# A network in six visits: half of the hidden width for one block of tokens at a time

## The chip, the cores and the metric

One core of a Trainium2 chip runs the kernel. Its engines are TensorE (PE; its weight loads are listed as PEld), VectorE (DVE), ScalarE (ACT), GpSimd (POOL) and SyncE (SP, which here issues nearly all transfers). The metric is the device time of one execution in microseconds (us), lower is better. Times of parts come from one profiled execution, counted from the start of its span.

## What is computed

Attention with a threshold, then eight experts of which each token takes one, then one network shared by all tokens:

```python
def _moe_ref(x, expert_emb, tau, w1, w2):            # N, D, E, F = (2304, 512, 8, 1024)
    ...
    for e in range(E):
        mask = expert_idx == e
        h = np.maximum(x[mask] @ w1[e], 0.0)
        out[mask] = gate_w[mask, None] * (h @ w2[e])
    return out.astype(np.float32)

def _moe2_ref(x, w_in, w_out, alpha):                # d_model, d_ff = 512, 2048
    h = x @ w_in
    g = np.maximum(h, 0.0) + alpha * np.minimum(h, 0.0)
    return (g @ w_out).astype(np.float32)
```

The weights of the experts and of the network arrive as 64-bit floats. Every matrix product is made of three with halves of lower precision (high x high, high x low, low x high), so most operands are split into a high and a low half.

## The kernel before

**Stages.** Attention runs to 349 us, the experts to about 625, the network to the end. The experts go step by step (`g` from 0 to 64, eight steps to an expert): a step loads staged weights `stg`, splits them (`wsplit`, L1118 to L1133), and multiplies (`l`, activation `h`, output `y`). An expert's result leaves as `yT` to `yt_d` in DRAM.

**The network's data.** Its hidden width of 2048 is 16 chunks of 128, `f`, in 8 pairs, `i`. A pair isn't multiplied directly: seven products, `PROD` = 1, 2, 6, 7, 5, 3, 4, of combined weights with combined tokens take the place of eight. The combined weights ("factors") of all 8 pairs are made in the experts, which leave DVE and POOL some room: `conv` converts half a pair of `w_in` (ScalarE L1594, DVE L1596 to L1605, POOL L1611), `sums` makes four sums on POOL (L1646 to L1649), and `factor` splits each of the seven (ScalarE L1661, POOL L1662) and stores it to `ws` in DRAM, 56 stores of 256 KB. `y2["early"]` gives the step `g` at which each is written out. The tokens' combinations come from `diff` (L1692 to L1698) and `split` (ScalarE L1683 high, DVE or POOL L1684 low) out of `raw`, read back by `fetch` from `yt_d`.

**The network's order.** Three blocks of 768 tokens (`q`), each in two halves (`hf`), go through all 8 pairs: 24 iterations. An iteration makes the seven products in two banks, `ha` and `hb` (L1759), each from weights `wr` loaded from `ws` one iteration ahead. `held` copies `ha` on ScalarE (L1764: v, w, d) since the bank goes on to be added to; `act` adds it to `hb` on DVE (`c`, L1773) and applies the activation, in block 0 by two ScalarE operations (L1777, L1778) and a join on DVE (L1785), later by two on DVE (L1782, L1783); then ScalarE makes the high half `gh` (L1789) and POOL the low half `gl` (L1790). `f2mm` multiplies the chunk's `gh` and `gl` with `w_out` (L1817 to L1819) into six banks `o`, between the products of the next iteration. After a block's last pair, `evac` scales the six banks by the gate into `os` (four buffers, ScalarE L1829 and DVE L1827), and `put` stores them to the tokens' rows (POOL, L1833).

**Conversions in the network.** `w_out` has 16 chunks; one is converted in the experts, 15 in block 0, one each four `cstep` calls, on the same engines with POOL L1616 and L1617 at the end.

**Order.** Each engine runs its instructions as written; `after`, `tick` and `cstep` in the text place the secondary work between products.

## Time and profile before

| | us |
|---|---|
| Median of three runs (1050.13 to 1053.92) | 1052.05 |
| The profiled execution | 1048.41 |
| Its span | 1046.5 |
| Attention, from the span's start | 349 |
| Experts, about | 276 |
| Network and end, about | 421 |

The profiled execution's time holds 1.9 us around its span. In rows of a timeline the columns are start, duration, engine, line, operation, output and inputs, and in brackets the engine's idle time ahead of it with what ended that; the duration of merged rows holds all of them. Matmuls overlap, so their starts tell more than their durations. In groups by line, "xN" is the count, then the busy time and the mean of one in ns.

### The profile page before, as it was taken

How to read it: one execution, taken by the hardware profiler on the slowest of the kernel's cores; microseconds unless marked ns; L12 is line 12 of the kernel's file. 1: busy time of each engine (PE TensorE's matmuls, PEld its weight loads, DVE VectorE, ACT ScalarE, POOL GpSimd, SP SyncE). 2: the span in 40 equal slices, each digit the busy share in tenths (PEclk: the TensorE clock that was granted, in tenths of full speed). 3: DMA queues.
4: the chain of work that ended last, by engine and by line, in shares of the span. 5: the costliest groups of instructions: out<-in, count | busy, mean ns of one | idle time of the engine just before them, and what ended most of it. 6: DMA issues, size and time to landing. Idle time of an engine off the chain costs nothing.

```text
span 1046.5 us, 18304 instructions
## 1 busy us (share of the span) xinstructions
PE 972.2 (93%) x6099; PEld 900.1 (86%) x6099; DVE 765.9 (73%) x1426; ACT 590.6 (56%) x1373; POOL 642.4 (61%) x640
## 2 busy tenths in 40 slices
PE   7999999899998699998998978998889999999995
PEld 6999999899997699998988966887778899889984
DVE  7999999999999588888886737866766434754342
ACT  6899999799996446665555535554452221422121
POOL 6988898899997226667875645654564222532223
PEclk9999999999999799999989989998989999999998
DMA  3333547533541766999999577554445334453331
GB/s 80 103 88 85 158 128 211 153 100 107 152 143 41 284 233 236 299 321 257 263 253 266 161 229 190 205 171 151 134 139 171 113 118 157 155 158 111 115 82 64
DMA packets 117049, 172.29 MB, mean 165 GB/s; under 512 B 23737, under 2 KB 57529, under 8 KB 116945
## 3 DMA queue, kind: packets, MB, share of 16 engines
q1 hardware_dynamic: 113344, 161.43, 52.4%
q0 software_dynamic: 3456, 9.46, 2.4%
q8 instruction: 51, 0.84, 0.3%
q14 instruction: 54, 0.43, 0.1%
q10 hardware_dynamic: 144, 0.13, 0.0%
HBM read 119.09 MB, written 43.04 MB: 155 GB/s over the span
## 4 chain that ended last, share of the span: by engine, by line
PE 53%; DVE 16%; issue 8%; DMA 8%; ACT 7%; POOL 7%; SPq 0%; POOLq 0%; ACTq 0%; DVEq 0%
PE ha L1759 7%; PE hb L1759 6%; PE s L622 5%; PE o L1819 5%; PE o L1818 5%; PE o L1817 5%; PE t L658 4%; DMA stg<-in_moe_w_dram 4%; PE l L1220 4%; DVE p L645 2%; DVE mx L629 2%; PE v L702 2%; PE m L721 2%; PE v L703 2%; PE y L1252 2%
## 5 line engine op out<-in xcount | busy, mean ns | idle before, releaser
L1790 POOL TENSOR_TENSOR gl<-c,gh 128x384 fp32r<-128x384 f32 x96 | 106.7, 1114 | 221.6 <-ACT gh L1789 134.2
L441 POOL TENSOR_TENSOR ptl<-x,pth 128x512 fp32r<-128x512 f32 x97 | 124.8, 1287 | 6.8
L1759 PE MATMUL ha<-x,wr 128*128 128x384 f32 x576 | 118.4, 341 | 4.4 <-ACT c L1778 2.8
L645 DVE SCALAR_TENSOR_TENSOR p<-s,mx,e 128x576 f32<-128x576 f32 x144 | 116.6, 812 | 7.2 <-ACT e L638 3.2
L1220 PE MATMUL l<-x,w 128*128 128x256 f32 (+6 forms) x744 | 121.4, 313 | 0.0
L1759 PEld LDWEIGHTS ha<-x,wr 128*128 128x128 f32 x576 | 104.1, 189 | 13.6 <-ACT c L1778 3.3
L1819 PE MATMUL o<-wo,gl 128*128 128x512 f32 x288 | 115.3, 400 | 0.4 <-POOL gl L1790 0.4
L1818 PE MATMUL o<-wo,gh 128*128 128x512 f32 x288 | 115.2, 400 | 0.0
L629 DVE TENSOR_REDUCE mx<-s 128x1 f32<-128x576 f32 x144 | 108.5, 754 | 8.1 <-PE s L622 5.1
L1220 PEld LDWEIGHTS l<-x,w 128*128 128x128 f32 x744 | 113.7, 193 | 0.6
L1817 PE MATMUL o<-wo,gh 128*128 128x512 f32 x288 | 114.1, 396 | 0.0
L658 PE MATMUL t<-ident,p 128*128 128x128 f32 (+1 forms) x720 | 111.8, 276 | 2.2 <-ACT x L684 0.9
L638 ACT ACTIVATE e<-s,mx 128x576 f32<-128x576 f32 x144 | 106.3, 739 | 6.6 <-DVE mx L629 6.0
L1759 PE MATMUL hb<-x,wr 128*128 128x384 f32 x432 | 91.1, 347 | 15.3 <-DVE c L1773 15.3
L1251 PE MATMUL y<-h,w 128*128 128x256 f32 (+6 forms) x256 | 84.9, 332 | 11.2 <-ACT h L1203 7.3
L1759 PEld LDWEIGHTS hb<-x,wr 128*128 128x128 f32 x432 | 78.3, 194 | 18.7 <-DVE c L1773 18.1
L1252 PE MATMUL y<-h,w 128*128 128x256 f32 (+6 forms) x256 | 82.7, 323 | 6.4 <-DVE h L1204 6.2
L658 PEld LDWEIGHTS t<-ident,p 128*128 128x128 f32 (+1 forms) x720 | 80.8, 137 | 8.3 <-ACT x L684 2.2
L622 PE MATMUL s<-ks,qs 128*128 128x288 f32 x256 | 82.7, 338 | 2.9 <-ACT qs L529 1.4
L1789 ACT CAST gh<-c 128x384 fp32r<-128x384 f32 x96 | 49.1, 511 | 62.3 <-DVE c L1783 55.7
L1253 PE MATMUL y<-h,w 128*128 128x256 f32 (+6 forms) x256 | 81.5, 318 | 0.0
L1773 DVE TENSOR_TENSOR c<-hb,d 128x384 f32<-128x384 f32 x24 | 13.4, 557 | 91.4 <-ACT d L1764 91.4
(252 smaller groups left out, 2568.1 us busy)
## 6 DMA issues: line engine op xcount, KB each, us to landing
wr<-ws SPq DMA_DIRECT2D x168, 256.0 KB
stg<-in_moe_w_dram SPq DMA_DIRECT2D x34, 512.0 KB
stg<-in_moe_w_dram SPq DMA_DIRECT2D x15, 1024.0 KB
ws<-wr SPq DMA_DIRECT2D x56, 256.0 KB
kx<-ks SPq DMA_DIRECT2D x60, 144.0 KB
xd<-zt SPq DMA_DIRECT2D x33, 256.0 KB
raw<-in_moe_w_in_dram SPq DMA_DIRECT2D x16, 512.0 KB
raw<-in_moe_w_out_dram SPq DMA_DIRECT2D x16, 512.0 KB
```

The costliest lines, as they stand in the source:

```text
L441: lambda: nc.gpsimd.tensor_tensor(lo, raw, hi.bitcast(F32), op=ALU.subtract))
L622: nc.tensor.matmul(s[:, hf, 0:288], lt, st[nm, a][:, hf * 288:(hf + 1) * 288], start=(j == 0 and x == 0), stop=(j == n - 1 and x == 1))
L629: nc.vector.tensor_reduce(out=mx[:, 0:1], in_=st["s", t][:, :, 0:288], op=ALU.min, axis=AX.XY)
L638: nc.scalar.activation(e, st["s", t][:, :, 0:288], AF.Exp, bias=st["mx", t][:, 0:1], scale=-1.0)
L645: nc.vector.scalar_tensor_tensor(out=p.rearrange("q (a b) -> q a b", a=2), in0=st["s", t][:, :, 0:288], scalar=st["mx", t][:, 2:3], in1=st ...
L658: nc.tensor.transpose(m[0:w, j * n + i * 128:j * n + (i + 1) * 128], st["p", t][:, c * 128:c * 128 + w], ident)
L1220: nc.tensor.matmul(m[:, 0:n], w[:, a, c], st["x"][:, b, c, 0:n], start=(i == 0), stop=(i + 1 == len(terms)))
L1759: nc.tensor.matmul(m, w[:, a, k], x[:, b, k], start=start and n == 0, stop=n + 1 == len(terms), skip_group_check=not start)
L1790: nc.gpsimd.tensor_tensor(gl, c, gh.bitcast(F32), op=ALU.subtract)
L1817: nc.tensor.matmul(m, gh[:, ts], WO[f][:, 0, :], start=(n[0] == 1), stop=False)
L1818: nc.tensor.matmul(m, gh[:, ts], WO[f][:, 1, :], start=False, stop=False)
L1819: nc.tensor.matmul(m, gl[:, ts], WO[f][:, 0, :], start=False, stop=(n[0] == KF2))
```

## The change

**Visits.** The network runs in six visits: block 0, 1, 2 with pairs 0 to 3, then block 2, 1, 0 with pairs 4 to 7, again 24 iterations with the same products. Between the two visits of block 2 the tokens stay; for blocks 0 and 1 the first visit's banks are scaled and stored in DRAM as `part` (12 stores of 256 KB), and read back and added in the second. The token block moves four times in place of two.

**Weights.** In the experts only pairs 0 to 3 get their factors; for 4 to 7 the converted `w_in` is stored as `wa_d` (four stores of 512 KB), and visits 1 to 3 load it and make the factors (`factors`: four sums on DVE, seven high halves on ScalarE, seven low ones on POOL, seven stores, with a ring `wf` of three tiles). Of `w_out`, four chunks are converted in the experts, four in visit 0 and eight in visits 1 to 3 (`wout`). `wr` has six buffers in place of eight, loaded five products ahead.

**Experts.** Conversions come every 2.6 steps in place of 3.4, with scratch tiles of the token pool; low halves of `w2` go to POOL every second step in place of every fourth; the fetch of block 0 stands ahead of step 54, its splits spread from step 56 on. `yt_d` holds two d-chunks of a token side by side, so a token's run is longer, and `split` reads every second word.

**A scheduler in the source.** Secondary steps are chains: a list of steps, each with an engine and a rough cost. After each product and each `f2mm`, `tick` gives every engine room and writes out what fits, at most one engine's steps of a chain at a time; "N" is an empty step, "W" a condition, "S" a transfer. `finish` writes out the rest of a chain where its result is due.

```diff
-CVG = {False: [17 * i // 5 for i in range(KF2 + 1)], True: [4 * i for i in range(15)] + [59, 61]}
+CVG = {False: [21 * i // 8 for i in range(KF2 + 4)], True: [4 * i for i in range(15)] + [59, 61]}
...
-NR = 8
-AHEAD = {0: 0, 4: 1, 5: 2, 6: 3, 7: 4}
+NR = 6
+VISITS = ((0, 0), (1, 0), (2, 0), (2, 1), (1, 1), (0, 1))
+NV = 4
+NQH = NP // 2
+NWO = 12
...
-    yt_d = dram.tile([128, KD, NT + CAPS_NEAR[0]], F32, name="yt_d")
+    yt_d = dram.tile([128, 2, NT + CAPS_NEAR[0], KD // 2], F32, name="yt_d")
+    wa_d = dram.tile([NQH, 128, 2 * DM], F32, name="wa_d")
+    part = dram.tile([4 * HT, 128, DM], F32, name="part")
...
-            eng = nc.gpsimd if not general and which == 2 and g % 4 == 1 and g > 8 else nc.vector
+            eng = nc.gpsimd if not general and which == 2 and g % 2 == 1 and g > 8 else nc.vector
...
-        def factor(i, p, eng):
-
-            t, flat, home = wtile(i, p)
+        def factor(i, p):
+
+            t, flat, home = wtile(y2["wf"], "wf", i, p)
             src = SUM[i][p]
             hi, lo = (t[:, x].rearrange("p (k j) -> p k j", k=2) for x in range(2))
             nc.scalar.copy(hi, src)
-            eng.tensor_tensor(lo, src, hi.bitcast(F32), op=ALU.subtract)
+            yield
+            nc.gpsimd.tensor_tensor(lo, src, hi.bitcast(F32), op=ALU.subtract)
+            yield
             nc.sync.dma_start(home, flat)
 
...
-            nc.sync.dma_start(t.rearrange("p (k n) -> p k n", k=KD), yt_d[:, :, n0:n0 + HB])
+            nc.sync.dma_start(t.rearrange("p (a n) -> p a n", a=2), yt_d[:, :, n0:n0 + HB, :].rearrange("p a n b -> p a (n b)"))
...
+            src = src.rearrange("p (n k) -> p k n", k=KD // 2)
+            XS[p] = t = pools[p].tile([128, 2, KD // 2, HB], F32R, tag=f"x{p}", name=f"x{p}")
...
+        for i in range(NQH):
+            g0 = 10.5 * i + 4.0
+            at(g0, lambda i=i: y2.update(sm=sums(i, WA[i])))
+            for x in range(4):
+                at(g0 + 0.5 * x, lambda x=x: y2["sm"][x](G))
+            for x, p in enumerate((1, 2, 4, 6, 7, 5, 3)):
+                f = run(lambda i=i, p=p: factor(i, p))
+                for y in range(3):
+                    at(g0 + 2.2 + 1.1 * x + 0.5 * y, f)
...
+        at(53.1, lambda: fetch(0, 0))
+        at(53.2, lambda: fetch(0, 1))
+        g0 = 56.0
+        for x, (kind, p, e) in enumerate((("s", 1, V), ("d", 1, G), ("s", 2, G), ("d", 3, V), ("d", 2, G), ("s", 7, V),
+                                          ("s", 6, V), ("s", 5, G), ("d", 4, G))):
...
+        for x in range(NR - 1):
+            at(59.0 + 0.7 * x, weights)
...
-        os_p = npool("os", bufs=4)
+        os_p = npool("os", bufs=2 * HT)
...
+        y2["wf"] = npool("wf", bufs=3)
...
+        def chain(order, steps, name=None, later=0):
+            chains.append({"order": (order, now[0]), "steps": list(steps), "at": now[0] + later, "name": name})
+            chains.sort(key=lambda c: c["order"])
+
+        def finish(name):
+            for x in [c for c in chains if c["name"] == name]:
+                while x["steps"]:
+                    x["steps"].pop(0)[2]()
+                if x in chains:
+                    chains.remove(x)
...
+        def tick(us):
+
+            now[0] += 1
+            for e in room:
+                room[e] = min(room[e] + us, 1.2)
+            for x in list(chains):
+                last = None
+                while x["steps"] and x["at"] < now[0]:
+                    e, cost, fn = x["steps"][0]
+                    if last not in (None, e) or room.get(e, 1) <= 0 or e == "W" and not fn():
+                        break
+                    x["steps"].pop(0)
+                    if e == "W":
+                        continue
+                    fn()
+                    if e in room:
+                        room[e] -= cost
+                    last = e
+                    if e == "N":
+                        break
+                if last is not None:
+                    x["at"] = now[0]
+                if not x["steps"] and x in chains:
+                    chains.remove(x)
+
...
+        def prod(v, i, p, m, start):
+            finish(("x", p))
...
                                  skip_group_check=not start)
+            if y2["wnext"][0] < len(y2["wseq"]):
+                vv, ii, _ = y2["wseq"][y2["wnext"][0]]
+                finish(("f", VISITS[vv][1] * NQH + ii))
+            y2["weights"]()
...
+            if v < 3:
+                first = [("A", 0.5, lambda: A.activation(u, m, AF.Relu, scale=-1.0)),
+                         ("A", 0.5, lambda: A.activation(c, m, AF.Relu))]
+                join = [("V", 0.87, lambda: V.scalar_tensor_tensor(
+                    out=c, in0=u, scalar=y2["na"][:, f:f + 1], in1=c, op0=ALU.mult, op1=ALU.add))]
...
+            chain(0, first + join + [("A", 0.52, halves), ("P", 1.12, low)], ("g", v, f, hf), 1)
...
+        def evac(v, hf, j, m):
+            q, h = VISITS[v]
+            tt = (2 * q + hf) * HT + j
+            g = y2["gs"][:, tt, 1:2].bitcast(F32)
+            last = v == NVIS - 1
+            loaded = h and q != VISITS[2][0]
+            if loaded:
+                o = O.pop(("part", tt))
+                V.scalar_tensor_tensor(out=o, in0=m, scalar=g, in1=o, op0=ALU.mult, op1=ALU.add)
...
+            if h:
+                if last:
+                    put(tt, o)
+                else:
+                    chain(1, [("P", 1.28, lambda: put(tt, o))])
...
+                chain(1, [("S", 0, lambda: nc.sync.dma_start(part[tt], o))], ("part", tt))
...
+        def partial(v, hf):
+            q, h = VISITS[v]
+            for j in range(HT):
+                tt = (2 * q + hf) * HT + j
+                finish(("part", tt))
+                O["part", tt] = o = os_p.tile([128, DM], F32, tag="os", name="os")
+                nc.sync.dma_start(o, part[tt])
...
+                finish(("g", v, f, hf))
+                finish(("wo", f))
...
+            kinds = [("V", 0.75), ("V", 0.75), ("V", 1.2), ("A", 0.65), ("V", 0.5), ("V", 0.75), ("P", 1.55), ("P", 1.4)]
+            chain(3, [("W", 0, lambda: len(open_) < 2), ("S", 0, load)] + [("N", 0, nothing)] * 3 + [("A", 0.67, begin)]
+                  + [(e, t, lambda k=k: nth(k + 1)) for k, (e, t) in enumerate(kinds)], ("wo", c))
...
+        def factors(i):
+
+            x = {}
+
+            def load():
+                made.append(i)
+                x["wa"] = wa = y2["wa"].tile([128, 2, DM], F32, tag="wa", name="wa")
+                nc.sync.dma_start(wa.rearrange("p x n -> p (x n)"), wa_d[i - NQH])
+
+            def nth(k):
+                if k == 0:
+                    x["sums"] = y2["sums"](i, x["wa"])
+                x["sums"][k](V)
+
+            def next_(k):
+
+                if k < 7:
+                    x[k] = t, _, _ = y2["wtile"](y2["wf"], "wf", i, PROD[k])
+                    A.copy(t[:, 0].rearrange("p (k j) -> p k j", k=2), SUM[i][PROD[k]])
+                    did("A", 0.42)
+                if 1 <= k < 8:
+                    h, l = (x[k - 1][0][:, y].rearrange("p (k j) -> p k j", k=2) for y in range(2))
+                    P.tensor_tensor(l, SUM[i][PROD[k - 1]], h.bitcast(F32), op=ALU.subtract)
+                if k >= 2:
+                    nc.sync.dma_start(x[k - 2][2], x[k - 2][1])
+                if k == 8:
+                    made.remove(i)
+
+            steps = [("W", 0, lambda: not made), ("S", 0, load)] + [("N", 0, nothing)] * 3
+            steps += [("V", 0.8, lambda k=k: nth(k)) for k in range(4)] + [("N", 0, nothing)]
+            for k in range(9):
+                steps += [("P", 0.95, lambda k=k: next_(k)), ("N", 0, nothing)]
+            chain(4, steps, ("f", i))
...
+                    chain(2, [("S", 0, lambda: fetch(VISITS[v + 1][0], 0)), ("S", 0, lambda: fetch(VISITS[v + 1][0], 1))]
+                          + [("N", 0, nothing)] * 5 + [("P", 2.15, lambda: diff(1, P)), ("V", 1.0, lambda: diff(3, V)),
+                                                       ("P", 2.15, lambda: diff(2, P))], "fetch")
...
+        work = {0: [("o", NV + x, x) for x in range(NQH)], 1: [("f", NQH, 0), ("f", NQH + 1, 2)] + [("o", 8 + x, x) for x in range(3)],
+                2: [("f", NQH + 2, 0), ("f", NQH + 3, 2), ("o", 11, 0), ("o", 12, 3)], 3: [("o", 13, 0), ("o", 14, 1), ("o", 15, 2)]}
...
+                if (v, i) != (NVIS - 1, NQH - 1):
+                    f2mm(v, (f0,), 0)
+        f2mm(v, (f0,), 1)
+        f2mm(v, (f1,), 1)
+        f2mm(v, (f0, f1), 0)
```

**DVE in the network's first iterations.** In before (`f<-f`, `f<-raw,f`, `r` are the five operations of a conversion; `c<-hb` is the addition, `c<-u,na,c` the join):

```order
L1773 TENSOR_TENSOR c<-hb,v 128x384
L1596 TENSOR_SCALAR f<-f 128x512
L1598 TENSOR_SCALAR f<-f 128x512
L1600 SCALAR_TENSOR_TENSOR f<-raw,f 128x512
L1785 SCALAR_TENSOR_TENSOR c<-u,na,c 128x384
L1604 TENSOR_SCALAR r<-f 128x512
L1605 SCALAR_TENSOR_TENSOR r<-raw,r 128x512
L1773 TENSOR_TENSOR c<-hb,d 128x384
L1785 SCALAR_TENSOR_TENSOR c<-u,na,c 128x384
```

and after, in the first visit, where `cr` is the raw `w_out`:

```order
L1891 TENSOR_TENSOR c<-hb,v 128x384
L1613 TENSOR_SCALAR r<-f 128x512
L1614 SCALAR_TENSOR_TENSOR r<-cr,r 128x512
L1897 SCALAR_TENSOR_TENSOR c<-u,na,c 128x384
L1606 TENSOR_SCALAR f<-f 128x512
L1607 TENSOR_SCALAR f<-f 128x512
L1891 TENSOR_TENSOR c<-hb,d 128x384
L1609 SCALAR_TENSOR_TENSOR f<-cr,f 128x512
L1897 SCALAR_TENSOR_TENSOR c<-u,na,c 128x384
L1613 TENSOR_SCALAR r<-f 128x512
L1891 TENSOR_TENSOR c<-hb,w 128x384
L1897 SCALAR_TENSOR_TENSOR c<-u,na,c 128x384
```

The three long operations of a conversion, which stood in a row, stand in two pieces with an addition or a join between.

**ScalarE where the last factors are due,** before in an iteration of block 1:

```order
L1764 COPY v<-ha 128x384
L1789 CAST gh<-c 128x384
L1764 COPY w<-ha 128x384
L1789 CAST gh<-c 128x384
L1764 COPY d<-ha 128x384
L1789 CAST gh<-c 128x384 x2
```

and after, in the third iteration of visit 3 (`wf` are the high halves of pair 7's factors):

```order
L1878 COPY v<-ha 128x384
L1913 CAST gh<-c 128x384
L2041 CAST wf<-wa 128x256 x2
L2041 CAST wf<-sum 128x256 x4
L2041 CAST wf<-wa 128x256
L1878 COPY w<-ha 128x384
L1913 CAST gh<-c 128x384
```

Seven copies have come in between the copies "v" and "w" of one iteration, in one piece.

**POOL at the end,** before:

```order
L1790 TENSOR_TENSOR gl<-c,gh 128x384 x3
L1833 DMA out_dram<-os,gs 2304x512 x6
L1790 TENSOR_TENSOR gl<-c,gh 128x384 x31
L1833 DMA out_dram<-os,gs 2304x512 x6
```

and after:

```order
L1950 DMA out_dram<-os,gs 2304x512
L1918 TENSOR_TENSOR gl<-c,gh 128x384 x11
L1950 DMA out_dram<-os,gs 2304x512 x3
L1918 TENSOR_TENSOR gl<-c,gh 128x384
L1950 DMA out_dram<-os,gs 2304x512 x3
```

One low half, which stood ahead of all six indirect stores, now stands behind three of them.

## Rows read from the trace of the kernel before

**Rows 1.** Busy time by stretch: start, end, length, each engine's busy us, granted clock, DMA.
```profile
460.00:600.00 140.00, 130.06 (x870) 125.88 (x869) 112.86 (x170) 76.70 (x181) 98.65 (x94) 0.95 0.92 248
...
608.00:615.00 7.00, 0.41 (x4) 0.17 (x2) 1.82 (x3) 2.90 (x6) 0.88 (x2) 0.71 1.03 307
...
640.00:776.00 136.00, 123.72 (x573) 108.01 (x573) 100.81 (x127) 69.99 (x145) 77.59 (x60) 0.95 0.50 168
776.00:905.00 129.00, 126.94 (x621) 113.89 (x622) 65.49 (x101) 34.62 (x68) 45.45 (x41) 0.99 0.45 139
```

**Rows 2.** Waits of TensorE, 349 to 640 us: total us, times, longest.
```profile
PE y L1251 <- ACT h L1203: 7.3, 2, 6.6
...
PE y L1251 <- ACT yT L1259: 3.9, 1, 3.9
```

**Rows 3.** Waits of TensorE, 640 us to the end.
```profile
PE hb L1759 <- DVE c L1773: 14.6, 7, 3.2
```

**Rows 4.** Timeline of TensorE in the network.
```profile
625.52 1.22 PE L1759 MATMUL ha<-x,wr 128*128 128x384 f32 x6
...
640.99 1.72 PE L1759 MATMUL ha<-x,wr 128*128 128x384 f32 x6 [2.85 <-ACT c L1778]
...
708.78 1.23 PE L1759 MATMUL ha<-x,wr 128*128 128x384 f32 x6
...
717.40 2.29 PE L1759 MATMUL hb<-x,wr 128*128 128x384 f32 x6 [3.22 <-DVE c L1773]
...
730.80 1.23 PE L1759 MATMUL ha<-x,wr 128*128 128x384 f32 x6
...
790.32 1.20 PE L1759 MATMUL ha<-x,wr 128*128 128x384 f32 x6
...
996.48 1.23 PE L1759 MATMUL ha<-x,wr 128*128 128x384 f32 x6
...
1012.19 1.23 PE L1759 MATMUL ha<-x,wr 128*128 128x384 f32 x6
...
1025.82 0.39 PE L1817 MATMUL o<-wo,gh 128*128 128x512 f32 x1
...
1033.79 0.39 PE L1819 MATMUL o<-wo,gl 128*128 128x512 f32 x1
```

**Rows 5.** Groups by line and shape, 640 us to the end.
```profile
L1785 DVE SCALAR_TENSOR_TENSOR c<-u,na,c 128x384 f32<-128x384 f32 x30 | 23.1, 771 | 8.1 <-ACT c L1778 7.9
...
L1773 DVE TENSOR_TENSOR c<-hb,v 128x384 f32<-128x384 f32 x23 | 12.7, 553 | 23.4 <-PE hb L1759 22.1 <-POOL gl L1790 0.9 <-ACT v L1764 0.4
...
L1605 DVE SCALAR_TENSOR_TENSOR r<-raw,r 128x512 f32<-128x512 uint32 x14 | 9.7, 692 | 0.5
...
L1616 POOL TENSOR_TENSOR f<-f,wo 128x512 f32<-128x512 f32 x14 | 19.0, 1357 | 0.0
```

**Rows 6.** Groups by line and shape, 363 to 626 us.
```profile
L1662 POOL TENSOR_TENSOR wr<-sum,wr 128x256 fp32r<-128x256 f32 x32 | 32.5, 1030 | 4.8 <-ACT wr L1661 4.5 <-issue 0.3
...
L1661 ACT CAST wr<-sum 128x256 fp32r<-128x256 f32 x32 | 12.7, 414 | 5.5 <-POOL sum L1647 5.5
```

**Rows 7.** The chain that ended last, 600 to 760 us: start, us, what.
```profile
598.00 8.17 DMA raw<-yt_d
...
629.34 10.16 DMA raw<-in_moe_w_out_dram
...
702.70 2.77 DMA wr<-ws
...
747.85 4.83 DMA wr<-ws
```

**Rows 8.** One of the splits, by line and shape, 640 us to the end.
```profile
L1684 DVE TENSOR_TENSOR x<-raw,x 128x768 fp32r<-128x768 f32 x8 | 10.5, 1332 | 7.1 <-ACT x L1683 7.1
```

**Rows 9.** Timelines of POOL and DVE at the end.
```profile
1038.47 0.97 POOL L1833 DMA_INDIRECT out_dram<-os,gs  x1 [0.57 <-ACT os L1829]
...
1034.72 0.75 DVE L1827 TENSOR_SCALAR os<-o,gs 128x512 f32<-128x512 f32 x1 [2.47 <-DMA out_dram<-os,gs]
```

More of the change, by code (lines that the diff above doesn't have):

```diff
@@ L1509, in experts @@
         ba = iter(()) if general else bases()
-        ahead, early = y2["ahead"], y2["early"]
+        early = y2["early"]
         todo = []
@@ new lines, in conv @@
+            steps = [x[2] for x in cvsteps(CV.pop((which, c)), f, r, hl)]
+            for group in ((0,), (1, 2, 3), (4,) if hl is not None else ()):
+                for x in group:
+                    steps[x]()
+                if group:
+                    yield
+            for x in steps[5 if hl is not None else 4:]:
+                x()
+            cvload()
+            if hl is None:
+                i, half = divmod(c, 2)
+                yield
+                if half == 0:
+                    WA[i] = y2["wa"].tile([128, 2, DM], F32, tag="wa", name="wa", bufs=2)
+                nc.gpsimd.tensor_tensor(WA[i][:, half], f.bitcast(F32), r.bitcast(F32), op=ALU.add)
+                if half and i >= NQH:
+                    yield
+                    nc.sync.dma_start(wa_d[i - NQH], WA.pop(i).rearrange("p x n -> p (x n)"))
@@ L1823, in evac, with low @@
-        def evac(tt, m, odd):
-            o = os_p.tile([128, DM], F32, tag="os", name="os")
-            g = y2["gs"][:, tt, 1:2].bitcast(F32)
-            if odd:
-                nc.vector.tensor_scalar(out=o, in0=m, scalar1=g, scalar2=None, op0=ALU.mult)
-            else:
-                nc.scalar.activation(o, m, AF.Copy, scale=g)
-            late.append(lambda: put(tt, o))
+                A.copy(gh, c)
+                G[v, f, hf] = gh, gl
+            def low():
+                gh, gl = G[v, f, hf]
+                P.tensor_tensor(gl, c, gh.bitcast(F32), op=ALU.subtract)
@@ new lines, in f2mm @@
+        def f2mm(v, fs, hf):
+            if v < 0:
+                return
+            q, h = VISITS[v]
+            joined = q == VISITS[2][0]
+            n = O.setdefault((q, hf), [0])
+            full = KF2 if joined else KF2 // 2
+            gs = []
+            for f in fs:
+                finish(("g", v, f, hf))
+                finish(("wo", f))
+                gs.append((f, *G.pop((v, f, hf))))
+            first, n[0] = n[0] == 0, n[0] + len(fs)
+            for j in range(HT):
+                if first:
+                    n.append(ps_o.tile([128, 512], F32, tag="o", name="o"))
+                m = n[1 + j]
+                ts = slice(j * 128, (j + 1) * 128)
+                for x, (f, gh, gl) in enumerate(gs):
+                    nc.tensor.matmul(m, gh[:, ts], WO[f][:, 0, :], start=first and x == 0, stop=False)
+                    nc.tensor.matmul(m, gh[:, ts], WO[f][:, 1, :], start=False, stop=False)
+                    nc.tensor.matmul(m, gl[:, ts], WO[f][:, 0, :], start=False, stop=n[0] == full and x + 1 == len(gs))
+                if n[0] == full:
+                    evac(v, hf, j, m)
+            if n[0] == full:
+                O.pop((q, hf))
+            tick(2.08 * len(fs))
@@ new lines, in xdiff_after_six @@
+        def xdiff_after_six():
+            chain(2, [("N", 0, nothing)] * 2 + [("P", 2.15, lambda: (finish(("x", 6)), diff(4, P)))], ("d", 4))
+        work = {0: [("o", NV + x, x) for x in range(NQH)], 1: [("f", NQH, 0), ("f", NQH + 1, 2)] + [("o", 8 + x, x) for x in range(3)],
+                2: [("f", NQH + 2, 0), ("f", NQH + 3, 2), ("o", 11, 0), ("o", 12, 3)], 3: [("o", 13, 0), ("o", 14, 1), ("o", 15, 2)]}
+        xsplit(3, "V")
+        xsplit(4, "V")
+        for v, (q, h) in enumerate(VISITS):
+            for i in range(NQH):
+                pair = h * NQH + i
+                f0, f1 = 2 * pair, 2 * pair + 1
+                if i:
+                    pv, g0, g1 = v, f0 - 2, f1 - 2
+                else:
+                    pv = v - 1
+                    pp = VISITS[pv][1] * NQH + NQH - 1
+                    g0, g1 = 2 * pp, 2 * pp + 1
+                for kind, x, when in work.get(v, ()):
+                    if when == i:
+                        (wout if kind == "o" else factors)(x)
+                if h and q != VISITS[2][0] and i == NQH - 2:
+                    partial(v, 1)
+                if h and q != VISITS[2][0] and i == NQH - 1:
+                    partial(v, 0)
```

428 lines of the change are left out of this document (216 added, 212 removed).

## The prediction

> **What bounds the kernel now.** I read four views, in this order. The table of busy time by stretch comes first, to see which part has room. Up to 349 us (attention) the change touches nothing. Of the rest, the experts (349 to 625) run with the DMA engines nearly full (0.92 from 460 to 600) and TensorE idle for 10 us there; one 7 us stretch, from 608 to 615, has TensorE busy for 0.41 us only [rows 1]. In the network the DMA engines are half used (0.50, 0.45), and TensorE is idle mostly in its first third: 12.3 us of 136, then 2.1 of 129 [rows 1]. So the experts are bound by what they load, with a hole at the hand-over, and the network by TensorE with waits early.
>
> Second, the waits of TensorE say who is late. In the experts it is the activation (7.3 us in two, one of them the hole) and the copies that empty the output banks (3.9) [rows 2]; in the network DVE's first addition of an iteration, `c`, 14.6 us in seven waits [rows 3].
>
> Third, the timeline of TensorE gives the network's loss, by the starts of its iterations. A quiet one takes 1012.19 - 996.48 = 15.71 us. The network starts at 625.52 and its last matmul at 1033.79, so it ends near 1034.1: 408.6 us against 24 x 15.71 = 377.0, a loss of 31.6 us [rows 4]. The last 36 matmuls (512 wide) start 0.228 apart, 35 spacings in 1033.79 - 1025.82 = 7.97 us; so the 36 of an iteration take 8.2 and its 42 narrow ones the other 7.5, six of them 1.07. The first nine iterations carry the loss: 790.32 - 625.52 = 164.8 against 9 x 15.71 = 141.4, less 27 x 0.228 = 6.2 (the first has no work of a predecessor), so 29.6 [rows 4]. A wait costs more than itself: the iteration from 708.78 to 730.80 lost 6.3 us, while TensorE stood 3.22; right after, six matmuls take 2.29 instead of 1.23 [rows 4]. I count 1.5 to 2 times each wait for that reason.
>
> Fourth, the operations: the conversions of `w_out` are what fills DVE and POOL there. an activation's addition takes 0.55 us and its join 0.77 on DVE; of a conversion's five operations there the last takes 0.69, and POOL's first 1.36 [rows 5]. Before puts three of the five back to back, and the other two right ahead of a `c` for which TensorE waits.
>
> **The change part by part.** The time is worked out against the profiled run, 1048.41 us; the median of the runs is 3.6 above it.
>
> *Network, iterations without special events.* Matmuls are the same in number and shape. `w_out` conversions come one or two DVE operations at a time between the `c` additions, as the order of DVE shows. DVE's sum for an iteration in the first two visits comes to 10 to 12 us (three additions and four joins at 0.55 and 0.77 [rows 5], conversions, splits), below 15.71, so a clump no longer sets the pace. I give each of the 19 iterations without an event 0.3 us: 6 us.
>
> *First iteration.* Before it took 640.99 - 625.52 = 15.47 us, where 15.71 - 6.2 = 9.5 would do: 6.0 lost [rows 4]. The chain shows why: a `raw` of `w_out` that landed after 10.16 us [rows 7], and its conversion on ScalarE ahead of an activation. After puts three empty steps between load and conversion, so ScalarE isn't held; 2 us (0.6 if all is hidden, 6 if not).
>
> *Moves of the token block.* Four instead of two. The second move of before cost at most the 2.1 us that TensorE was idle from 776 to 905 [rows 1]; after starts both loads ahead of the last iteration: 1.5 each, 6 us (0 to 12).
>
> *`w_out` chunk 7 (visit 1, first iteration).* It is four operations short when its product comes, and `finish` writes them out there. Behind p2 DVE must do `c` 0.55, a join 0.77, then two more at up to 0.69, then POOL one of 1.36 [rows 5]: some 4 us during which TensorE stands; with the slower matmuls 6 (2 to 7).
>
> *Factors of pair 7 (visit 3, third iteration).* `finish` writes seven ScalarE copies in one piece, ahead of `held` "w", through a ring of three tiles. Copy 3 waits for copy 0 (0.41), its low half (1.03) [rows 6] and its store; copy 6 for the same again. No row shows a store of 256 KB in the network; the nearest are loads of 256 KB there, 2.77 and 4.83 us [rows 7]. With 2.77, twice (0.41 + 1.03 + 2.77) = 8.4 us of ScalarE, plus "w" itself and two operations before; TensorE reaches the product that needs "w" 7.3 us after it has done p1 (three products of 1.07 and eighteen wide matmuls): a wait of 2.3, with 4.83 of 6.4. I take 4 with the slow matmuls (2 to 9). Stores stand on SP ahead of 26 loads of `wr`, but those are five products early.
>
> *The rest of the factors and the partial sums.* 28 stores of 256 KB leave the experts; what SP issues in the network grows from 52.7 to 71.0 MB, counted in its order. With half of the DMA time free there [rows 1], I take the 18.3 MB at nothing; what hides them is the five products by which `wr` is loaded ahead. Without that cover they would be 18.3 MB at the 168 GB/s of 640 to 776 [rows 1], 109 us, all on the path; the nearest row, TensorE idle for 2.1 of 129 us with 0.45 of the DMA time used [rows 1], is far nearer to nothing. The last conversion, just before visit 4: 0.5.
>
> So the network loses 6 + 2 + 6 + 6 + 4 + 0.5 = 24.5 against 31.6: 7 us won (bounds: 12 to 36 lost).
>
> *Experts.* DVE gets three conversions more and 14 low halves fewer, POOL 28 factor lows (1.03 [rows 6]) and 16 sums fewer and 14 low halves more: both no longer. SP's order shows equal bytes between the `yt_d` stores up to about step 45, so 460 to 540 stays as it is; after that there are fewer. The hole at 608 to 615 comes out of the fetch of the first block (8.17 us in the chain [rows 7]), then the splits, ahead of the last activations on ScalarE. After fetches two to three steps earlier and spreads the splits over seven. The hole is 6.6 us [rows 2], some 10 with the slow matmuls behind it; I count 7 of these as won, and 2 of a 3.9 us wait for the copies that empty the banks [rows 2]: 9 us (3 to 17).
>
> *End of the network.* From the end of the last product (T = 1025.82 [rows 4]) before needs 8.3 us to its last matmul's end, and 20.7 to the end of the span at 1046.5, the last put being issued at 1038.47 [rows 9] and the end 8.0 later. After does the same 36 matmuls, but POOL's order puts three indirect stores, each waiting for DVE's evacuation, ahead of the low half that the last two products need: a wait of about 3 us, and 1.5 for the low half of f0. Six buffers instead of four take away the 2.47 that DVE waited for one [rows 9]. The last put comes at T + 14.2, the end at T + 22.2: 1.5 lost (from 2 won to 3 lost).
>
> Sum: 1048.4 - 7 - 9 + 1.5 = 1033.9; with the 3.6 to the median **1037 us**.
>
> **Where a page is weighed.** A row first: a load of 256 KB took 2.77 us in the chain at 702 us, and 4.83 in another place [rows 7]. The Trainium skill, "DMA: Bandwidth & Descriptors", section "Anatomy of one DMA", gives 2.0 us fixed plus bytes over 436 GB/s, by its figures an estimate of 2.6 us for such a store; by it the ring of three never waits at a regular pace, and rival C below falls away.
>
> The other: no row shows an element-wise operation that reads every second word. The Trainium skill, "SBUF — State Buffer", in its note on SBUF cachelines, has 16-byte lines with full speed from two hits a line, so a step of 8 bytes would be free, and rival D would not occur.
>
> **The rivals.**
>
> *A. Nearly all is covered.* The two `finish` waits and the moves hide, and the waits from 540 to 565 go as well. For it: the SP and DVE orders are lighter after step 45. Against: two chains are visibly unfinished at their due place. Network loss 15, experts 14 won: 1048.4 - 16.6 - 14 + 1.5 + 3.6 = 1023.
>
> *B. The experts gain nothing and the new waits eat up the network's gain.* For it: 0.92 DMA share up to 600 [rows 1], and the same loads; the hole would then stand a little later, as the activations still share ScalarE with the splits. 1048.4 - 2 + 1.5 + 3.6 = 1051.5.
>
> *C. Slower: the ring of three factor tiles holds ScalarE.* In visits 1 to 3, 28 factor copies stand between ScalarE's `held` copies, and 25 of them wait until the store three tiles back has landed. Copies are two steps apart, 2.9 us, and a store is written out one copy before its tile is wanted, so ScalarE waits L - 2.9, L being the time to landing. `held` has some 2 us of slack, and it decides from L = 5 or so. Loads of 256 KB at 2.77 and 4.83 speak against it; 8.17 and 10.16 of larger transfers in a loaded stretch for it [rows 7]. At L = 6.5, 25 x 1.6 = 40 us: no gain is left, 1037 + 30 (some of these waits overlap others) = 1067.
>
> *D. The new layout is dear.* `split` then reads every second word. If that doubled its operations (DVE's takes 1.33 [rows 8]), four moves of seven splits each would each be some 4 us late: 1037 + 16 = 1053.
>
> **How the numbers follow.** The forecast 0.50, A 0.17, B 0.13, C 0.13, D 0.07. About 0.3% (1048.9 to 1055.2) is what a measurement of this kernel can tell from no change. B and D have their centre inside that band, with tails on both sides. Faster: 0.50 + 0.17 + 0.05 (of B and D) = 0.72; same: 0.11 (of B and D); slower: 0.13 + 0.04 = 0.17. The forecast's own bounds, all terms at their ends, are 1020 and 1057, and the likely part of that 1028 to 1046. The range 1018 to 1058 takes in most of A, all of B and D, and leaves out C and the best end of A.
>
> **What would show it.** Right: the stretch of 7 us without TensorE before the network is below 3 us; iterations of the first visit take 15.7 to 16.5; one wait of 3 to 5 us for POOL's `wo` or DVE in the first iteration of visit 1, and one for ScalarE's "w" in the third of visit 3; last put 14 us after the last `hb`. Wrong: many short waits of TensorE for `held` copies in visits 1 to 3, with ScalarE idle before L2041 for a DMA (C); splits above 1.0 us on ScalarE (D); the 460 to 560 stretch longer than before.

## The result: 1.1% slower, and the time went into the experts

The changed kernel took 1063.05 us (median of four, 1062.39 to 1063.82) where the kernel before took 1051.1 beside it: a ratio of 1.011, with a 95% interval of 1.0087 to 1.0133. In a later set on one chip it took 1061.34 against 1041.68, 1.0174 (1.014 to 1.0209); the kernel before was 9 us shorter there, the changed one 2, and why isn't known. So the sets are compared by their ratios. The profiled span is 1060.6 us against 1046.5, 14.1 longer. I had forecast 1037 with a range to 1058: wrong in the sign.

The busy time by stretch, in the columns of [rows 1] (start, end, length, busy us of PE, PEld, DVE, ACT and POOL, granted clock, DMA share, GB/s):

```profile
349.00:460.00 111.00, 99.54 (x587) 94.61 (x587) 76.53 (x131) 48.91 (x107) 41.58 (x34) 0.94 0.73 243
460.00:600.00 140.00, 122.22 (x780) 115.61 (x778) 103.91 (x164) 70.20 (x159) 89.99 (x79) 0.95 0.72 236
600.00:640.80 40.80, 40.80 (x295) 40.34 (x295) 26.93 (x35) 21.37 (x45) 18.97 (x11) 1.00 0.56 165
640.80:776.00 135.20, 125.12 (x608) 110.58 (x607) 93.79 (x110) 79.37 (x158) 82.74 (x60) 0.96 0.61 194
776.00:905.00 129.00, 123.07 (x602) 109.74 (x600) 80.36 (x110) 61.64 (x130) 73.37 (x67) 0.97 0.66 212
905.00:1060.60 155.60, 138.68 (x668) 121.24 (x666) 82.79 (x119) 37.94 (x72) 71.43 (x61) 0.97 0.47 150
```

and the first of these stretches in the kernel before:

```profile
349.00:460.00 111.00, 109.97 (x688) 107.07 (x689) 87.67 (x151) 60.71 (x136) 49.89 (x44) 0.97 0.82 271
```

From 349 to 460 us TensorE is busy 99.54 us, where it was 109.97, and from 460 to 600 us 122.22, where it was 130.06 [rows 1], although the DMA engines are *less* used: 0.73 and 0.72, not 0.82 and 0.92. The stretch ahead of the network, where [rows 1] had 0.41 us of 7, is now full (40.80 of 40.80): the hole at 608 is gone, as forecast. But the network starts late. The starts of some of its iterations and its longest waits:

```profile
640.85 1.21 PE L1869 MATMUL ha<-x,wr 128*128 128x384 f32 x6
...
647.83 1.28 PE L1869 MATMUL ha<-x,wr 128*128 128x384 f32 x6 [1.57 <-DMA wr<-ws]
...
650.64 1.28 PE L1869 MATMUL hb<-x,wr 128*128 128x384 f32 x6 [1.53 <-DMA wr<-ws]
...
653.85 1.21 PE L1869 MATMUL ha<-x,wr 128*128 128x384 f32 x6
...
702.00 1.22 PE L1869 MATMUL ha<-x,wr 128*128 128x384 f32 x6
...
707.34 0.79 PE L1985 MATMUL o<-wo,gh 128*128 128x512 f32 x1 [2.95 <-ACT wo L1612]
...
711.81 0.80 PE L1986 MATMUL o<-wo,gh 128*128 128x512 f32 x1 [3.67 <-POOL wo L1618]
...
727.42 1.21 PE L1869 MATMUL ha<-x,wr 128*128 128x384 f32 x6
...
869.79 1.23 PE L1869 MATMUL ha<-x,wr 128*128 128x384 f32 x6
...
883.41 2.29 PE L1869 MATMUL ha<-x,wr 128*128 128x384 f32 x6 [5.08 <-ACT w L1878]
...
892.55 0.69 PE L1869 MATMUL ha<-x,wr 128*128 128x384 f32 x3
...
1022.63 1.21 PE L1869 MATMUL ha<-x,wr 128*128 128x384 f32 x6
...
1046.77 0.50 PE L1987 MATMUL o<-wo,gl 128*128 128x512 f32 x1 [3.13 <-POOL gl L1918]
```

The network starts at 640.85 us in place of 625.52 [rows 4]: 15.3 lost. From there to the start of the last iteration it loses 26.6 us against 23 quiet iterations (1022.63 - 640.85 = 381.8, against 23 x 15.71 - 6.2 = 355.1), where before lost 31.6: 5 won. From the end of the last product to the end of the span it takes 24.3 us in place of 20.7: 3.6 lost. Together 15.3 - 5 + 3.6, the 14 us of the spans.

Who is late in the experts? TensorE's waits there, with total, times and longest, then ScalarE's:

```profile
PE y L1257 <- ACT h L1209: 21.4, 9, 4.1
PE y L1258 <- DVE h L1210: 4.9, 8, 1.4
```

```profile
ACT h L1209 <- PE l L1226: 67.5, 36, 3.8
ACT wf L1696 <- DMA ws<-wf: 60.7, 15, 9.3
```

TensorE's waits for the activation `h` have risen from 7.3 us in two [rows 2] to 21.4 in nine. And ScalarE, which makes `h`, stands 60.7 us in fifteen waits ahead of L1696, the high half of a factor, until a *store* of 256 KB has landed. L1696 writes a tile of the pool `wf`, which has two tiles in the experts (`y2["wf"] = mpool("wf", bufs=2)`, a line that the diff above leaves out; the factors of before went through the eight tiles of `wr`). One such wait, from the timelines of ScalarE, POOL, SP and TensorE:

```profile
489.82 0.41 ACT L1696 CAST wf<-wa 128x256 fp32r<-128x256 f32 x1
492.95 0.42 ACT L1696 CAST wf<-wa 128x256 fp32r<-128x256 f32 x1
...
506.98 0.41 ACT L1696 CAST wf<-wa 128x256 fp32r<-128x256 f32 x1 [9.34 <-DMA ws<-wf]
...
492.74 1.23 POOL L1698 TENSOR_TENSOR wf<-wa,wf 128x256 fp32r<-128x256 f32 x1
...
501.68 0.74 SPq L1700 DMA_DIRECT2D ws<-wf  x1
...
507.72 0.38 PE L1257 MATMUL y<-h,w 128*128 128x256 f32 x1 [3.68 <-ACT h L1209]
```

The copy at 489.82 us writes a tile; its low half starts on POOL at 492.74; the store is issued on SP at 501.68; the next copy but one, at 506.98, needs the tile and has waited 9.34 us. Behind it on ScalarE stands the activation `h`, and TensorE's `y` at 507.72 has waited 3.68 us for that. Worked out from such timelines, the way round (copy, low half, issue, landing) took 8 to 18 us over the fifteen waits, with a median of 12.6. The low half began up to 8.8 us after the copy had ended, and the store was issued up to 7.7 us after the low half; the store's own part, from issue to landing (min, median, max), is under half of the median:

```profile
DMA to landing us min/median/max: 3.4/4.6/7.4
```

### The profile page after: what moved, and what is told of

Same layout as the page of the kernel before. It is cut to its first block, busy times and chain, and to the rows that moved or that the text cites. A ratio compares the mean times of both kernels' runs of the same rounds, so it can differ in the third digit from the quotient of the medians.

```text
span 1060.6 us, 18417 instructions
## 1 busy us (share of the span) xinstructions
PE 977.0 (92%) x6099; PEld 900.1 (85%) x6099; DVE 785.4 (74%) x1431; ACT 619.9 (58%) x1419; POOL 682.7 (64%) x654
## 5 line engine op out<-in xcount | busy, mean ns | idle before, releaser
L1918 POOL TENSOR_TENSOR gl<-c,gh 128x384 fp32r<-128x384 f32 x96 | 111.3, 1161 | 158.2 <-ACT gh L1913 140.9
L1257 PE MATMUL y<-h,w 128*128 128x256 f32 (+6 forms) x256 | 84.5, 330 | 21.4 <-ACT h L1209 21.4
L1869 PE MATMUL hb<-x,wr 128*128 128x384 f32 x432 | 86.9, 335 | 2.0 <-DMA wr<-ws 1.5
L1869 PEld LDWEIGHTS hb<-x,wr 128*128 128x128 f32 x432 | 75.9, 188 | 3.1 <-issue 1.8
L707 PE MATMUL v<-pth,hlv 128*128 128x288 f32 (+2 forms) x256 | 75.2, 316 | 2.2 <-DVE run L953 1.0
```

Of the source, the lines that this page charges most:

```text
L1257: nc.tensor.matmul(m[:, 0:n], w[:, 0, dsl], h[:, 0, 0:n], start=(f == 0), stop=False)
L1869: nc.tensor.matmul(m, w[:, a, k], x[:, b, k], start=start and n == 0, stop=n + 1 == len(terms), skip_group_check=not start)
L1918: P.tensor_tensor(gl, c, gh.bitcast(F32), op=ALU.subtract)
```

## The experiments

Three theories of the experts stood against each other. **R**, the ring: two tiles are too few for the way round, and ScalarE, which must take its copies in order, holds the activations. **P**: POOL makes twice as many low halves of `w2`, loads of `stg` wait for it on SP, and hold what is behind them. **B**: more bytes, or the new layout. The kernel before took 1041.7 to 1044.3 us (medians) beside these runs; ratios are against it.

**Six tiles.** The factors of the experts go through the pool of `wr`:

```diff
-            y2["wf"] = mpool("wf", bufs=2)
...
-            t, flat, home = wtile(y2["wf"], "wf", i, p)
+            t, flat, home = wtile(wr_p, "wr", i, p)
```

> The kernel after, but the factors made in the experts go through the six tiles of wr (as before, where there were eight) in place of a pool of two. Theory R (the ring: ScalarE stands in its order ahead of a factor's copy until the store two tiles back has landed, 60.7 us in 15 waits in the experts, and the activations h behind it are late): these waits all but vanish, the network starts at 620 to 628 us in place of 640.9, the time is 1040 to 1047. Theory P (POOL makes twice as many low halves of w2, loads of stg on SP wait for it, 73.4 us, and hold all behind them): ScalarE's waits move to others, the network starts after 634, the time is over 1055. Theory B (more bytes or the new layout): no change, 1060 to 1064.

1029.66 us, ratio 0.9864 (0.9824 to 0.9904), 10 us below what R gave. Nothing of ScalarE's waits for stores is left; its longest in sum is the ordinary one, for TensorE, and TensorE is busy 134.02 of the 140 us that had 122.22:

```profile
ACT h L1208 <- PE l L1225: 91.2, 54, 3.5
```

```profile
349.00:460.00 111.00, 108.06 (x666) 104.46 (x667) 90.89 (x153) 57.84 (x127) 49.22 (x40) 0.97 0.80 275
460.00:600.00 140.00, 134.02 (x934) 129.02 (x933) 121.73 (x175) 79.13 (x178) 98.69 (x80) 1.00 0.77 259
```

The network starts at 608.8 us, 16.7 earlier than in before and earlier than any theory had it. Theory R stands. What follows beyond it: without the ring the change is faster than before.

**POOL's share as before.**

```diff
-            eng = nc.gpsimd if not general and which == 2 and g % 2 == 1 and g > 8 else nc.vector
+            eng = nc.gpsimd if not general and which == 2 and g % 4 == 1 and g > 8 else nc.vector
```

> The kernel after, but POOL again makes the low halves of w2 every fourth step, not every second. Theory R: ScalarE still waits 40 us or more for stores in the experts, the network starts at 634 to 643, the time is 1055 to 1064. Theory P: the network starts before 628, the time is 1040 to 1048. Theory B: 1060 to 1064.

1060.44 us, 1.0153 (1.0115 to 1.0192). SP's waits for POOL fall from 77.3 us in the changed kernel (the first line) to 34.5 here, and that changes next to nothing: ScalarE still waits 57.5 us.

```profile
SPq L1111 <- POOL w L1139: 77.3, 26, 6.3
```

```profile
ACT wf L1696 <- DMA ws<-wf: 57.5, 15, 8.9
...
SPq L1111 <- POOL w L1139: 34.5, 13, 5.6
```

Theory P falls as the main cause, and B too, since the six tiles move the same bytes in the same layout.

**Both.**

> Both edits. Theory R: within 4 us of the six-tile kernel alone. Theory P: within 4 us of the other alone. If each carries a part, it is faster than either by more than 4 us.

1026.11 us, 0.9837 (0.9797 to 0.9876): 3.5 below the six tiles alone, within the 4 us that R allowed. The intervals overlap, so that POOL's share costs anything is likely, not shown. The later experiments have this kernel as their base.

**The reverse: two tiles in the kernel before.**

```diff
-NR = 8
+NR = 7
...
+            y2["wf"] = mpool("wf", bufs=2)
...
-            t, flat, home = wtile(i, p)
+            t = y2["wf"].tile([128, 2, 256], F32R, tag="wf", name="wf")
+            flat, home = t.rearrange("p x n -> p (x n)").bitcast(F32), ws[i, PROD.index(p)]
```

> The kernel before, but its 56 factors go through a pool of two tiles in place of the eight of wr (wr keeps seven, as many as are loaded ahead). Theory R: ScalarE waits for stores 40 us or more in the experts, and the network starts 10 to 35 us later than 625.5: 1060 to 1085. Theories P and B: no change, 1048 to 1055.

1086.7 us, 1.0402 (1.0362 to 1.0443), just above R's range; the network starts at 666.75 us, 41 later than 625.5 and not 10 to 35. From there to the last product it takes as long as in before (399.9 and 399.3 us), so the tile that `wr` lost costs nothing. The same wait appears in a kernel that had none of it, in 29 places, with twice as many stores:

```profile
ACT wf L1663 <- DMA ws<-wf: 92.3, 29, 6.6
```

**Three tiles.** Every third factor takes a tile of `wr`, so a tile comes back after three.

```diff
+            third = (7 * i + (1, 2, 4, 6, 7, 5, 3).index(p)) % 3 == 2
-            t, flat, home = wtile(y2["wf"], "wf", i, p)
+            t, flat, home = wtile(*((wr_p, "wr") if third else (y2["wf"], "wf")), i, p)
```

> The kernel after, but every third factor in the experts takes a tile of wr, so that a copy needs the tile of the factor three back, not two. Copies are written 1.1 steps apart, some 5 us; from a copy to the landing of its store took 12 to 17 us where ScalarE waited. Two tiles leave 10 us, three 15, six 30. If the way round is compared with that depth: ScalarE's waits for stores fall from 60 us to between 5 and 25, and the time lies at 1030 to 1042, between the kernels with two and with six. If two tiles fail for another reason than depth: 1055 to 1064.

1035.15 us, 0.993 (0.9906 to 0.9954). ScalarE's waits are 10.9 us in four:

```profile
ACT h L1209 <- PE l L1226: 85.1, 48, 3.8
ACT wf L1697 <- DMA ws<-wf: 10.9, 4, 4.8
```

So 60.7, 10.9 and 0 us of waits for two, three and six tiles, with 1061, 1035 and 1030 us: it is the depth, against a way round of 8 to 18 us. (The three times are from three chips; the ratios to before are 1.0174, 0.993 and 0.9864.)

**Is it SP's queue that makes the way long?** The same two tiles, but POOL issues the store itself behind its low half.

```diff
-            nc.sync.dma_start(home, flat)
+            nc.gpsimd.dma_start(home, flat)
```

> The kernel after with its pool of two tiles in the experts, but those stores are issued by POOL itself, right behind its low half, and so don't stand on SP behind loads that wait. A store is written out some 5.5 us ahead of the copy that needs its tile, and landed in 3.4 to 7.4 us once issued. If the queue on SP is what makes the ring too short: ScalarE's waits fall from 60 to under 20 us, 1032 to 1042. If the landing alone is too long for two tiles: 40 us or more of waits stay, 1052 to 1064.

1064.11 us, 1.0212 (1.0187 to 1.0237):

```profile
ACT wf L1696 <- DMA ws<-wf: 59.8, 14, 9.0
```

No gain. The figures fall in with the second reading, or just above it, but its reason doesn't hold, since landing alone is 5 us of the way. SP's hold is another part (up to 7.7 us from low half to issue), and so is POOL, which got to the low half up to 8.8 us after the copy. Here the issue has moved from SP's queue into POOL's order, half a step behind the low half, and other work of POOL stands in between, which can itself wait for DVE:

```profile
493.14 1.22 POOL L1698 TENSOR_TENSOR wf<-wa,wf 128x256 fp32r<-128x256 f32 x1
499.06 1.29 POOL L1646 TENSOR_TENSOR wa<-x7s 128x512 f32<-128x512 f32 x1 [4.70 <-DVE x7s L1614]
...
501.56 0.56 POOL L1700 DMA_DIRECT2D ws<-wf  x1
```

From low half to issue it took up to 7.2 us in this kernel, nearly as long as on SP, and POOL got to the low half up to 10.6 us after the copy. Moving the issue alone didn't shorten a way that goes through several engines' orders; depth covers it.

**The network's own steps,** on the base of both edits. First the conversions of chunks 5 to 7, started one iteration earlier in visit 0:

```diff
-        work = {0: [("o", NV + x, x) for x in range(NQH)], 1: [("f", NQH, 0), ("f", NQH + 1, 2)] + [("o", 8 + x, x) for x in range(3)],
+        work = {0: [("o", NV + x, max(0, x - 1)) for x in range(NQH)], 1: [("f", NQH, 0), ("f", NQH + 1, 2)] + [("o", 8 + x, x) for x in range(3)],
```

> Base: six tiles and POOL's share as before (both edits; 1026 us). Here the conversions of w_out chunks 5, 6 and 7 start one iteration earlier in visit 0. In the base the fourth iteration and its hand-over take 24.7 us in place of 15.7, with waits of 3.0 and 4.0 us for chunk 7. If those waits are what costs: 9 us less, 1015 to 1020. Rival: visit 0 has no room, and the waits come back there as waits for additions on DVE: 1022 to 1027.

1025.55 us, no gain. The iteration after the hand-over to visit 1 fell from 24.7 to 22.1 us, but the network's first rose by 2.8, with a longer wait for a load of `wr`:

```profile
614.94 1.30 PE L1868 MATMUL hb<-x,wr 128*128 128x384 f32 x3 [2.82 <-DMA wr<-ws]
```

On SP two raw loads instead of one now go out ahead of seven loads of `wr`; that they cause it is likely, not shown. Neither reading was right: the time fits the rival's range, but the wait moved to a load and not to additions, and at the hand-over a wait of 3.7 us for chunk 7 stayed, its last POOL operation standing behind two `gl` that come late.

Then the factors of pairs 4 to 7 two or three iterations earlier (their chains start in the second iteration of visit 0, the first two of visit 1 and the first of visit 2; none is written out in one piece):

```diff
-        work = {0: [("o", NV + x, x) for x in range(NQH)], 1: [("f", NQH, 0), ("f", NQH + 1, 2)] + [("o", 8 + x, x) for x in range(3)],
-                2: [("f", NQH + 2, 0), ("f", NQH + 3, 2), ("o", 11, 0), ("o", 12, 3)], 3: [("o", 13, 0), ("o", 14, 1), ("o", 15, 2)]}
+        work = {0: [("o", NV + x, x) for x in range(NQH)] + [("f", NQH, 1)], 1: [("f", NQH + 1, 0), ("f", NQH + 2, 1)] + [("o", 8 + x, x) for x in range(3)],
+                2: [("f", NQH + 3, 0), ("o", 11, 0), ("o", 12, 3)], 3: [("o", 13, 0), ("o", 14, 1), ("o", 15, 2)]}
```

> The same base; the factors of pairs 4 to 7 start in the second iteration of visit 0, not in the first of visit 1, so that none is written out in one piece in visit 3. The iteration there took 22.3 us in place of 15.7, with a wait of 4.85 us for ScalarE's copy w. If the piece of seven copies is the cause: 6.5 us less, 1018 to 1021. If the ring of three tiles in the network holds ScalarE wherever the copies stand (the third rival of the prediction): the wait spreads over other iterations, 1024 to 1030.

1020.32 us, 0.9787 (0.9748 to 0.9825), as the first reading had it: the wait for ScalarE's copy "w" is gone from visit 3, whose third iteration falls from 22.3 to 15.7 us, and ScalarE waits 0.6 us for stores in the whole network. At this pace three tiles are enough. Some of the gain is lost again at the hand-over to visit 1, which takes 26.7 us in place of 24.7.

Then POOL's order at the end:

```diff
         f2mm(v, (f0,), 1)
+        for f in (f0, f1):
+            finish(("g", v, f, 0))
         f2mm(v, (f1,), 1)
```

> The same base; the low halves of the last two chunks are written out ahead of the last block's first three indirect stores on POOL. In the base TensorE waits 3.13 us there, and the end comes 24.3 us after the last product, against 20.7 in the kernel before. If POOL's order is the cause: 3 to 4 us less, 1021 to 1024. Rival: the three stores then set the end themselves: 1025 to 1027.

1022.03 us, 0.9802 (0.9769 to 0.9836), as expected. The last low half now stands ahead of the six stores:

```profile
1003.47 1.01 POOL L1917 TENSOR_TENSOR gl<-c,gh 128x384 fp32r<-128x384 f32 x1 [1.09 <-ACT gh L1912]
1006.09 0.99 POOL L1949 DMA_INDIRECT out_dram<-os,gs  x1 [1.62 <-DVE os L1930]
```

All three, with pair 4's factors from the first iteration on; and a last version in which chunk 7 is written out in visit 0's last iteration, the chunks starting in iterations 0, 1, 1 and 2:

```diff
+            if (v, i, p) == (0, NQH - 1, 7):
+                finish(("wo", NV + NQH - 1))
```

> The three edits together, the factors of pair 4 starting in the first iteration of visit 0. If they add: 1026 less 9, 6.5 and 3.5, so 1005 to 1010; if they take each other's room in visit 0, 1012 to 1018.

> Base of six tiles and POOL's old share, the earlier factors, POOL's order at the end, and chunk 7 of w_out written out in visit 0's last iteration ahead of its sixth product, the chunks starting in iterations 0, 1, 1, 2. If the place of chunk 7 in the orders was what was left: the hand-over to visit 1 takes under 18 us in place of 21, and the first iterations lose no more than the base: 1008 to 1013. If not: 1014 to 1018.

1015.52 us, 0.9743 (0.9706 to 0.9781), and 1014.34 us, 0.9727 (0.9703 to 0.9751). The edits add only in part. With all three the hand-over to visit 1 falls from 24.7 to 21.3 us, but the network's first iteration rises from 11.9 to 17.0, with a wait of 4.8 us for a load of `wr`. In the last version the first iteration takes 13.9 us, the hand-over 22.2, not under 18, and the iteration ahead of it 17.7 in place of 15.7. So the place of chunk 7 was not all that was left: TensorE's longest wait at the hand-over is still there, 3.9 us, now for POOL's `gl`, which stands behind a difference of tokens (2.16 us), a split (2.57) and a factor's low half (1.04) in POOL's order:

```profile
PE o L1986 <- POOL gl L1917: 5.8, 4, 3.9
```

That is the lowest median of the versions tried, not told apart from the one before it by their intervals: 2.7% below before, and 4.4% below the changed kernel by the ratios of one set (0.9727 against 1.0174). The changed kernel itself, run again in that set:

> The kernel after once more, for a comparison on one chip with the others of this set: 1.009 to 1.020 of before, with some 60 us of ScalarE's waits for stores in the experts.

1061.34 us, 1.0174, with ScalarE's waits for stores in the experts at 61.6 us.

## Why the prediction was wrong, point by point

**The step that failed** is the paragraph on the experts. It counted operations and bytes of each engine and found both no longer, and took 9 us as won; 15.3 were lost. It never asked how many tiles the factors have in their new place. The mechanism was in my hands: rival C is this very wait, ScalarE held in order by a ring of factor tiles until a store has landed. I put it into the network, where the ring has three tiles, and left out the experts, where it has two and the DMA engines are fuller. Two copies, each 1.1 steps apart, leave some 10 us; the way round took 12.6 at the median. Rows for a first estimate stood there: ScalarE's copy of 0.41 us and POOL's low half of 1.03 [rows 6] for the work, 8.17 and 10.16 us for larger transfers under load [rows 7] for the landing, together already some 10. But that sum would have come near by luck: the landing was 4.6 us at the median, and the rest was waiting in POOL's and SP's orders, for which no row shown before had a price. Of the 29 us by which the profiled run lies above the sum of 1033.9, 24 are in this one term. My last sign of being wrong did come: the work from 460 us on took longer (780 matmuls in the trace from 460 to 600 us, against 870).

**What I took for the bound** was wrong too, in that I read 0.92 of DMA share from 460 to 600 us [rows 1] as a wall that the change could not move. With six tiles TensorE was busy 134.0 of these 140 us, where before had 130.06, at a share of 0.77 and a granted clock of 1.00, where both before and the kernel with two tiles had 0.95; the trace has 934 of its matmuls there, against 870. Transfers were indeed waited for in before: ScalarE stood 40.2 us for staged weights in the experts (first line), with six tiles 2.5 (second line), and on the chain that ended last single loads of them took up to 11.7 us (third line), where the changed kernel's land after 4.3 and 6.1 at the median for the two sizes:

```profile
ACT w L1132 <- DMA stg<-in_moe_w_dram: 40.2, 15, 9.2
```

```profile
ACT w L1137 <- DMA stg<-in_moe_w_dram: 2.5, 4, 1.3
```

```profile
494.21 11.72 DMA stg<-in_moe_w_dram
```

So the loads did hold ScalarE, and the change, once the ring was out of the way, freed it. With six tiles the network started 16.7 us earlier than in before, at the upper end of my 3 to 17; which of the moved parts (half of the stores, the layout of `yt_d`, the earlier fetch) gave how much of that, these runs don't split.

**The network** came out nearly as worked out in sum, 26.6 us lost against 24.5, with its terms scattered:

- the first iteration 3.5 (2 forecast): 653.85 - 640.85 = 13.0 against 9.5, but not for the conversions that I had named: its two waits, 1.57 and 1.53 us, are for loads of `wr`, the one place where the five products of lead didn't cover them;
- `w_out` chunk 7: 727.42 - 702.00 = 25.4, so 9.7 (6 forecast, with a first move that I had counted apart), in two waits of 2.95 for ScalarE's half and 3.67 for POOL's;
- the factors of pair 7: 892.55 - 869.79 = 22.8, so 7.1 (4 forecast, 2 to 9 the range), with the wait for "w" of 5.08, where 2.3 to 6.4 had been worked out, and six matmuls in 2.29 behind it as in [rows 4]. In that piece ScalarE also stood 4.66 us for a low half, for which I had counted only its 1.03: on POOL it stood behind two steps of a `w_out` conversion (the line is below);
- the other moves with the last conversion some 5.5 (6.5);
- plain iterations 1.0 for all together (6): the spread conversions do work, and no wait for `c` is longer than 1.3 us.

The bounds were added too narrowly: with the network's 12 lost, 17 won in the experts and 2 at the end the sum is 1013, not 1020, and the network's own terms at their ends give 11 to 41 lost, not 12 to 36.

**Rival C in the network** did not happen at a regular pace. ScalarE's waits for stores there, in all 28 factors, and a store's time from issue to landing:

```profile
ACT wf L2041 <- DMA ws<-wf: 4.3, 5, 1.6
```

```profile
877.27 0.41 ACT L2041 CAST wf<-sum 128x256 fp32r<-128x256 f32 x1 [4.66 <-POOL wf L2045]
```

```profile
DMA to landing us min/median/max: 2.0/3.1/5.2
```

Of the 4.3 us, 3.7 lie in the one piece in which pair 7's copies were written out together, as does the wait of the second line. The bounds that I took, 2.77 and 4.83 us [rows 7], enclose the median of 3.1. The Trainium skill, "DMA: Bandwidth & Descriptors", section "Anatomy of one DMA", by whose figures 2.6 us was estimated, has its figures from transfers issued on GpSimd, and these are SP's: the network's median of 3.1 is near the estimate, the experts' 4.6 is not, nor the 5.1 of the stores that POOL issued; and it speaks of one transfer, not of the way round that decided.

**Rival D** did not happen either. A split that reads every second word takes 1.243 us at the mean on DVE, against 1.332 [rows 8], and on ScalarE 0.892, against 0.832:

```profile
L1743 DVE TENSOR_TENSOR x<-raw,x 128x768 fp32r<-128x768 f32 x13 | 16.2, 1243 | 1.3 <-ACT x L1741 1.3
...
L1741 ACT CAST x<-raw 128x768 fp32r<-128x768 f32 x17 | 15.0, 892 | 0.0
```

The Trainium skill, "SBUF — State Buffer", in its note on cachelines, by the prediction's reading has such a step free. The ScalarE rows are 7% longer, so nearly free; on DVE the shortest is 0.941 us, against 0.944, and the means differ both ways (those from `t` 1.497 against 1.159), so something else than the step sets them.

**The end** lost 3.6 us where 1.5 was forecast, by the mechanism named: the low half behind three stores on POOL, and TensorE's wait of 3.13 us for it (1046.77 in the timeline above):

```profile
1044.72 0.97 POOL L1950 DMA_INDIRECT out_dram<-os,gs  x1 [0.30 <-issue]
1045.71 1.01 POOL L1918 TENSOR_TENSOR gl<-c,gh 128x384 fp32r<-128x384 f32 x1
...
1052.67 0.97 POOL L1950 DMA_INDIRECT out_dram<-os,gs  x1 [1.18 <-POOLq L2281]
```

The low half at 1045.71 starts when the third store has been issued. The last put comes at 1052.67, 16.4 us behind the last product and not 14.2: after the wait the evacuations run one by one on DVE, and three stores start 2.2 us apart instead of 1.3. With the low halves ahead of the stores the end came 4.7 us sooner after the last product than in its base.

## What to carry to other kernels

For each pool whose tile goes out by a store, count the way round of a tile (writer, second writer in its own engine's order, issue, landing) and compare it with the number of tiles times the spacing of the writers. Count the waits in those orders too: here they were more of it than the landing. Where the way round is longer, the engine that writes first stops, with all that is behind it in its order. When work is moved, look at the size of the pool that it moves to before counting operations. A wait found by reasoning at one place should be looked for at each place where the same code runs, the most loaded one first.

## What was not expected of the hardware

A store issued from POOL's queue landed no sooner than from SP's: 5.1 us (2.5 to 7.6) against 4.5 (3.2 to 8.1) in the kernel beside it. And a ring of three tiles in place of two, 2 KB each in a partition, was worth 2.4% of the whole kernel (0.993 against 1.0174 of before), three more beyond it 0.7% (0.9864). The memory was there already: the third tile and the six are `wr`'s, which no load used until the last steps of the experts.
